# Turning pairs of fp16 as fp32 words, and setting the turns between matmuls, in a linear-attention and highway kernel

## The chip, the cores and the metric

The kernel runs on one core of a Trainium2 chip. A core has a matrix engine (TensorE, here PE, with its weight loads PEld), a vector engine (VectorE, DVE), a scalar engine (ScalarE, ACT), a general engine (GpSimd, POOL), a queue that issues transfers (SyncE, SP) and 16 DMA engines. The metric is the device time of one execution in microseconds, as the median of several runs.

## The reference

Eight batches of eight heads, 576 rows of 64 values each, go through linear attention; the result, 4608 rows of 512, goes through a highway layer with two 512 x 512 weights.

```
q_s = exp(q - max(q)) / sum(exp(q - max(q)))      # over the 64 values of a row
k_s = exp(k - max(k)) / sum(exp(k - max(k)))      # over the 576 rows
kv  = einsum('bhsd,bhse->bhde', k_s, v)
x   = einsum('bhsd,bhde->bhse', q_s, kv)          # then as 4608 rows of 512
H   = max(x @ w_h, 0)
T   = 1 / (1 + exp(-(x @ w_t + b_t)))
out = T * H + (1 - T) * x
```

Inputs and output are fp32.

## The kernel before

**Tiles.** The 4608 rows are cut into 36 tiles of 128 rows. Two batches make nine tiles: four of each batch, and one that holds the last 64-row groups of both. Tile numbers run from 0 to 35; tiles 31 to 34 belong to the last batch, number 7, and tile 35 to batches 6 and 7.

**Stages of a batch.** `ek` (ACT, line 253) writes exp(k) as fp16. `vc` (line 259) writes v as fp16, mostly on POOL. `kv` (line 269) multiplies them in 72 matmuls of 64 x 64 with 65 columns; the 65th column is a column of ones that gives the sum over rows. `kr` and `kn` (lines 281, 287) divide by that sum into a block matrix `kvb`. `eq` (ACT, lines 298 to 308) writes exp(q) as fp16 into `qe`, in the order position, head pair, value. `qt` (lines 310 to 327) turns `qe` on PE: a matmul of 128 columns with `is_transpose`, in which the data are the stationary operand, loaded by PEld, and an identity matrix is the moving one. The result goes to PSUM as fp16. `qc` (line 333) copies it to `eq`. Two of the three groups of batch 7 are turned by the DMA engines instead (`qd`, line 340).

**Stages of a tile.** `xu` (line 361): four matmuls of 130 columns of `eq` with `kvb`; two further columns carry the sums. `rs` and `x` (DVE, lines 370, 376) divide: `x` is the attention output, 128 rows of 512 in fp16. `xt` (line 384) turns `x` on PE, in four matmuls of 128 columns, each of which takes every second column of a block of 256; the result goes into the first half of the PSUM bank `turned`. `xe` (line 391) copies it to `xT`, on DVE or ACT. `bw` (lines 399, 401) puts the bias into a PSUM bank, by a copy on ACT or by a matmul. `mt` (line 411) adds x @ w_t to it and `mh` (line 419) forms x @ w_h, each in four matmuls of 512 columns with a quarter of `xT` as the stationary operand. `th` (lines 433, 435) is the gate's tanh on ACT; `dd` (DVE, line 439) forms max(x @ w_h, 0) - x in a scaled form (the identity is taken off w_h beforehand); `uu` multiplies, on DVE (line 453) or in two steps on POOL (lines 450, 451); `oo` adds x on POOL (line 471) and `st` stores.

Tiles 0, 4 and 5 take `xu`, `xt`, `xe` and the products in halves. At the start, `fill` runs matmuls on zeros (line 167) in the same bank `turned`.

**What sets the order.** A list of steps, `ORDER` (lines 16 to 62), names every step of the program, such as `xt_34_0` or `mh_34_0`; a suffix gives the engine. The loop at the end issues the steps in the list's order, and each engine works through its own part of them in that order; waits follow from the tiles that a step reads, writes or takes over. Loads and stores are all issued by SP but for three small ones, in that order too. Near the end the list reads (with "..." for steps left out):

```
xu_35_0 bw_32:A rs_35_0 oo_33_0 xt_34_0 mt_32_0 bw_34:A xe_34_0:D mh_34_0 st_33_0 x_35_0
xt_35_0 mt_34_0 dd_32 th_32_0 bw_35_1 oo_30_0 st_16_0 st_30_0 uu_32_0 xe_35_0 oo_32_0 mh_35_0
```

So on PE the turns of tile 34 are followed by the gate product of tile 32, and this by tile 34's own product `mh_34`, which needs the copy `xe_34`.

Of the kernel before, what the change touches and what calls it, by code (L numbers as in the profile page):

```python
# [8 lines left out]
FP32 = mybir.dt.float32  # L9
FP16 = mybir.dt.float16  # L10
AF = mybir.ActivationFunctionType
# [4 lines left out]
ORDER = """  # L16
# [49 lines left out]
def kernel(  # L66
# [10 lines left out]
    nc = tc.nc  # L77
    B, H, S, D = q.shape
    DM = H * D
    P = 128  # L80
    NP = 64
    NJ = S // NP
# [7 lines left out]
    qep = pool("qep", 2)  # L90
    eqp = pool("eqp", 4)
    xp = pool("xp", 6)
    xtp = pool("xtp", 3)
# [39 lines left out]
    def heads(i, k):  # L133
        return (k, k + 1) if i in HALVED else (0, 2)
# [39 lines left out]
    def landing(which, b):  # L174
        return once(f"{which}32{b}", lambda: ld.tile([P, 4, NJ * D], FP32, tag=which, name=f"{which}32_{b}"))
# [4 lines left out]
    def load_kv(which):  # L180
        def step(e, b, c):
            n = (2 if which == "k" else 1, 2)[b] if b < 2 else 4
            nc.sync.dma_start(landing(which, b)[:, c:c + n], rows_of(which, b)[:, c:c + n])
# [107 lines left out]

    GROUPS = ((0, 4), (4, 8), (8, 9))

    def eq(e, b, g):
        t = once(f"qe{b}", lambda: qep.tile([P, NJ, 4, D], FP16, tag="qe", name=f"qe_{b}"))
        if b in WIDE:
            if g == 2:
                nc.scalar.activation(t[:, 8], flat_q(b)[:, MAIN:].rearrange("p (c d) -> p c d", c=4), AF.Exp)
                return
            half = slice(0, 8) if e == "F" else slice(4 * g, 4 * g + 4)  # L300
            src = flat_q(b)[:, 0:MAIN].rearrange("p (c t d) -> p c t d", c=4, t=8)[:, :, half]
            nc.scalar.activation(t[:, half].rearrange("p t c d -> p c t d"), src, AF.Exp)
            return
        js, cs = slice(*GROUPS[g]), slice(0, 4)
        if b >= 2:
            js, cs = slice(0, NJ), slice(0, 4) if e == "F" else slice(2 * g, 2 * g + 2)
        nc.scalar.activation(t[:, js, cs].rearrange("p j c d -> p c j d"),  # L307
                             T[f"q32{b}"].rearrange("p c (j d) -> p c j d", j=NJ)[:, cs, js], AF.Exp)

    def qt(e, b, g):  # L310
        j0, j1 = GROUPS[g]
        a, s = (2, 2) if g < 2 else (1, 1)
        t = T[f"qps{b}_{g}"] = ps_q.tile([P, a, 4, s * NP], FP16, tag="qps", name=f"qps_{b}_{g}")
        if b in WIDE and g < 2:
            main = T[f"qe{b}"].rearrange("p j c d -> p (j c d)")[:, 0:MAIN]
            main = main.rearrange("p (hh j kk f) -> p j hh kk f", j=4, hh=2, kk=2)
            for jp in (2 * g, 2 * g + 1):
                for n in range(4):
                    nc.tensor.matmul(t[:, jp % 2, n], main[:, jp, n % 2, n // 2], idh,  # L319
                                     is_transpose=True, start=True, stop=True, skip_group_check=True)  # L320
            return
        for j in range(j0, j1):
            for kk in range(2):
                nc.tensor.matmul(  # L324
                    t[:, (j - j0) % 2, 2 * kk:2 * kk + 2].rearrange("p n (t s u) -> p n t s u", s=s, u=2)[:, :, :, (j - j0) // 2],
                    T[f"qe{b}"][:, j, 2 * kk:2 * kk + 2].rearrange("p c d -> p (c d)"), idh,
                    is_transpose=True, start=True, stop=True, skip_group_check=True)

    def qc(e, b, g):
        copy = nc.scalar.copy if e == "A" else nc.vector.tensor_copy  # L330
# [6 lines left out]
    def qd(e, b, g):  # L337
        t = T[f"eq{b}_{g}"] = eqp.tile([P, 2, 4, P], FP16, tag="eq", name=f"eq_{b}_{g}")
        half = MAIN // 2
        nc.sync.dma_start_transpose(t.rearrange("p a n t -> p (a n) t"),  # L340
                                    T[f"qe{b}"].rearrange("p j c d -> p (j c d)")[:, g * half:(g + 1) * half])
# [36 lines left out]

    def xt(e, i, k):
        k0, k1 = heads(i, k)  # L380
        t = T[f"xtps{i}"] = turned[:, 0]
        for n in range(2 * k0, 2 * k1):
            n0 = n // 2 * 2 * P
            nc.tensor.matmul(t[:, n], T[f"x{i}"][:, n0 + n % 2:n0 + 2 * P:2], idh, is_transpose=True,  # L384
                             start=True, stop=True, skip_group_check=True)

    def xe(e, i, k):
        k0, k1 = heads(i, k)
        t = once(f"xT{i}", lambda: xtp.tile([P, 4, P], FP16, tag="xT", name=f"xT_{i}"))
        copy = nc.vector.tensor_copy if e == "D" else nc.scalar.copy  # L390
        copy(t[:, 2 * k0:2 * k1], T[f"xtps{i}"][:, 2 * k0:2 * k1])  # L391


    def bw(e, i, h=0):
# [8 lines left out]
    def parts_of(i, k):  # L403
        return range(2 * k, 2 * k + 2) if i in HALVED else range(4)

    def mt(e, i, k):
        cs = columns(i, k)
        parts = parts_of(i, k)
        first = once(f"mt{i}", lambda: k) == k and len(parts) < 4
        for n in parts:  # L410
            nc.tensor.matmul(T[gate(i, k)][:, cs], T[f"xT{i}"][:, n], w16["t"][:, n, cs], start=False,  # L411
                             stop=(n == parts[-1] and not first), skip_group_check=True)

    def mh(e, i, k):
        first = f"gps{i}" not in T
        t = once(f"gps{i}", lambda: ps_g.tile([P, DM], FP32, tag="gps", name=f"gps_{i}"))
        parts = parts_of(i, k)
        for n in parts:
            nc.tensor.matmul(t, T[f"xT{i}"][:, n], w16["h"][:, n], start=(first and n == parts[0]),  # L419
                             stop=(n == parts[-1] and not (first and len(parts) < 4)), skip_group_check=True)  # L420


    LIFTED = {s.split(":")[0] for s in ORDER.split() if s.startswith("uu") and s[-2:] == ":P"}
# [49 lines left out]
    def st(e, i, h):  # L473
# [21 lines left out]
        setuppool=setup_pool, setupdve=setup_dve, bsplit=bsplit, fill=fill,  # L495
        k=load_kv("k"), v=load_kv("v"), q=load_q, w=load_w, b=load_b, bp=bp, bc=bc,
        wtc=wt_cast, whc=wh_cast, whd=wh_less_identity, ek=ek, vc=vc, kv=kv, kr=kr, kn=kn, eq=eq, qt=qt, qc=qc, qd=qd,
        xu=xu, rs=rs, x=x, xt=xt, xe=xe, bw=bw, mt=mt, mh=mh, th=th, dd=dd, uu=uu, oo=oo, st=st)
    with tc.manual_schedule():
        for step in ORDER.split():  # L500
            name, _, eng = step.partition(":")
            kind, *at = name.split("_")
            does[kind](eng, *(int(a) if a.isdigit() else a for a in at))


# [28 lines left out]
```

## Time and profile before

| | |
|---|---|
| median of 3 runs | 118.87 us (118.81 to 119.09) |
| span of the profiled execution | 116.9 us, 3424 instructions; no time of its own is listed beside the span |
| granted PE clock over the span | 0.995 |
| busy: PE, PEld | 109.5 us, 61.6 us |
| busy: DVE, ACT, POOL | 93.3, 90.0, 89.1 us |
| moved by DMA | 40.58 MB, 347 GB/s on the mean |
| turns on PE: of `x`, of queries | 144, and 80 + 48 |
| matmuls of the two products of 512 columns | 144 and 140 (and 8 of 256 columns) |

The span runs from the first to the last instruction of the program; what a run's time has beyond it lies before and after. Busy times of PE are those of overlapping matmuls: one that lasts 220 ns may be followed by the next after 55 ns. In a row of groups the fields are line, engine, operation, output <- inputs, shape and count, then the busy time and the mean of one in ns, then the idle time ahead of them with what ended it. In a timeline or a chain the first number is the start in us and the second the length.

### The profile page before, as it was taken

To read this page: it belongs to the slowest core of one execution; us is meant where nothing else is said; L and a number is where in the kernel's file an instruction comes from. 1 tells how busy PE (TensorE), PEld (TensorE's weight loads), DVE (VectorE), ACT (ScalarE), POOL (GpSimd) and SP (SyncE) were. 2 spreads that over 40 slices of the span, in tenths; PEclk is the share of its full clock that TensorE was granted. 3 is DMA by queue.
4 is the path that set the end of the run, shared out by engine and by line. 5 is a ranking of instruction groups with operands and counts; after the bars stand their busy time and mean duration, and the time that the engine had idled before them with its cause. 6 is when DMAs were issued, how large, how long until landed. Compare 5 with 4: busy or idle time off the path is not lost.

```text
span 116.9 us, 3424 instructions
## 1 busy us (share of the span) xinstructions
PE 109.5 (94%) x1351; PEld 61.6 (53%) x1351; DVE 93.3 (80%) x222; ACT 90.0 (77%) x132; POOL 89.1 (76%) x99
## 2 busy tenths in 40 slices
PE   5999987999999999999999999999999999999930
PEld 2354544545665656565665547566564555554520
DVE  5642587589799979979889798988989887899870
ACT  4356461897999999989999999998597998545520
POOL 5022237208996999999999999999989699999960
PEclk9999999999999999999999999999999999999998
DMA  2999999999999999999999999999999956992875
GB/s 42 399 392 377 408 398 385 375 377 379 393 391 397 383 391 393 358 375 387 357 376 360 387 392 363 390 381 383 399 398 217 302 204 270 397 404 115 315 295 179
DMA packets 24195, 40.58 MB, mean 347 GB/s; under 512 B 5362, under 2 KB 11762, under 8 KB 24180
## 3 DMA queue, kind: packets, MB, share of 16 engines
q1 hardware_dynamic: 24032, 40.24, 96.9%
q8 instruction: 10, 0.16, 0.6%
q10 hardware_dynamic: 148, 0.14, 0.4%
q14 instruction: 5, 0.04, 0.1%
HBM read 30.41 MB, written 9.44 MB: 341 GB/s over the span
## 4 chain that ended last, share of the span: by engine, by line
PE 67%; POOL 15%; issue 6%; DVE 5%; DMA 3%; SPq 1%; POOLq 0%; DVEq 0%
PE tps L411 18%; PE gps L419 16%; PE turned L167 9%; POOL o L471 7%; PE xu L361 6%; PE turned L384 5%; PE kv L269 5%; PE qps L324 4%; POOL u L451 4%; DMA out_dram<-o 3%; POOL g L450 2%; PE qps L319 2%; POOL v L259 2%; DVE x L376 2%; PE tps L401 1%
## 5 line engine op out<-in xcount | busy, mean ns | idle before, releaser
L471 POOL TENSOR_TENSOR o<-u,x 128x512 f32<-128x512 f16 (+1 forms) x36 | 40.6, 1143 | 1.6 <-DVE u L453 0.7
L411 PE MATMUL tps<-w16t,xT 128*128 128x512 f16 (+1 forms) x148 | 37.3, 373 | 0.0
L419 PE MATMUL gps<-w16h,xT 128*128 128x512 f16 x144 | 36.8, 379 | 0.5 <-DVE xT L391 0.5
L376 DVE TENSOR_TENSOR x<-xu,rs 128x512 f16<-128x512 f32 (+1 forms) x39 | 25.2, 649 | 2.4
L259 POOL CAST v<-v 128x1152 f16<-128x1152 f32 (+1 forms) x14 | 14.0, 1010 | 14.7 <-DMA v<-in_v_dram 13.7
L439 DVE SCALAR_TENSOR_TENSOR d<-x,gps 128x512 f16<-128x512 f16 x36 | 24.5, 680 | 0.3
L451 POOL TENSOR_TENSOR u<-g,d 128x512 f16<-128x512 f16 x17 | 19.7, 1158 | 1.7 <-DVE rs L370 0.4
L253 ACT ACTIVATE ek<-k 128x576 f16<-128x576 f32 (+2 forms) x15 | 17.9, 1225 | 3.0 <-DMA k<-in_k_dram 3.0
L419 PEld LDWEIGHTS <-xT 128*128 128x128 f16 x144 | 13.0, 98 | 12.3 <-DVE xT L391 1.8
L399 ACT COPY tps<-ball 128x512 f32<-128x512 f32 x28 | 16.6, 597 | 3.5 <-DVE u L453 3.2
L411 PEld LDWEIGHTS <-xT 128*128 128x128 f16 x148 | 13.2, 98 | 10.6 <-DVE xT L391 0.4
L361 PE MATMUL xu<-kvb,eq 128*128 128x130 f16 (+1 forms) x160 | 14.8, 224 | 0.2 <-DVE kvb L287 0.2
L384 PE MATMUL turned<-idh,x 128*128 128x128 f16 x144 | 14.2, 220 | 0.5 <-DVE x L376 0.5
L391 DVE COPY xT<-turned 128x512 f16<-128x512 f16 (+1 forms) x28 | 10.9, 391 | 4.2 <-PE turned L384 3.0
L435 ACT ACTIVATE tps<-tps 128x512 f32<-128x512 f32 (+1 forms) x20 | 11.2, 559 | 3.6 <-PE tps L411 3.3
L453 DVE SCALAR_TENSOR_TENSOR u<-tps,d 128x512 f16<-128x512 f32 (+1 forms) x19 | 12.7, 671 | 1.4 <-ACT tps L435 0.6
L361 PEld LDWEIGHTS <-eq 128*128 128x128 f16 (+1 forms) x160 | 10.0, 100 | 7.3 <-DVE x L376 2.5
L167 PE MATMUL turned<-blank 128*128 128x512 f16 x40 | 12.4, 458 | 1.5 <-POOL blank L149 1.3
L384 PEld LDWEIGHTS <-x 128*128 128x128 f16 x144 | 9.8, 98 | 6.0 <-DVE x L376 2.1
L307 ACT ACTIVATE qe<-q 128x1024 f16<-128x1024 f32 (+3 forms) x9 | 9.4, 1052 | 4.1 <-DMA q<-in_q_dram 4.1
L450 POOL TENSOR_SCALAR g<-th 128x512 f16<-128x512 f16 x17 | 10.6, 621 | 0.9 <-ACT th L433 0.9
L433 ACT ACTIVATE th<-tps 128x512 f16<-128x512 f32 x17 | 10.0, 594 | 0.9 <-PE tps L411 0.9
(48 smaller groups left out, 106.8 us busy)
## 6 DMA issues: line engine op xcount, KB each, us to landing
k<-in_k_dram SPq DMA_DIRECT2D x6, 1152.0 KB, 12.2
v<-in_v_dram SPq DMA_DIRECT2D x6, 1152.0 KB, 12.0
out_dram<-o SPq DMA_DIRECT2D x23, 256.0 KB, 4.0
q<-in_q_dram SPq DMA_DIRECT2D x10, 512.0 KB, 11.5
out_dram<-o SPq DMA_DIRECT2D x6, 512.0 KB, 3.8
k<-in_k_dram SPq DMA_DIRECT2D x4, 576.0 KB, 9.3
q<-in_q_dram SPq DMA_DIRECT2D x2, 1152.0 KB, 14.2
q<-in_q_dram SPq DMA_DIRECT2D x2, 640.0 KB, 10.5
```

Of the source, the lines that this page charges most:

```text
L167: nc.tensor.matmul(spare, blank[:, 0:P], blank, start=True, stop=True, skip_group_check=True)
L253: nc.scalar.activation(t[:, :, c:c + n].rearrange("p j c d -> p c j d"), T[f"k32{b}"][:, c:c + n].rearrange("p c (j d) -> p c j d", j=NJ), ...
L259: copy(v16[b % NV][:, c:c + n, :, 0:D], T[f"v32{b}"][:, c:c + n].rearrange("p c (j d) -> p c j d", j=NJ))
L361: nc.tensor.matmul(dst, turned_q(b, jp, n), kvb[b % NKV][:, hh, kk], start=True, stop=True, skip_group_check=True)
L376: nc.vector.tensor_mul(t[:, k0:k1], sums(i, k)[:, :, :, 0:64], T[f"rs{i}_{k}"][:, 0:k1 - k0].unsqueeze(3).to_broadcast([P, k1 - k0, 4, D]))
L384: nc.tensor.matmul(t[:, n], T[f"x{i}"][:, n0 + n % 2:n0 + 2 * P:2], idh, is_transpose=True, start=True, stop=True, skip_group_check=True)
L399: nc.scalar.copy(t[:, cs], ball[:, cs])
L411: nc.tensor.matmul(T[gate(i, k)][:, cs], T[f"xT{i}"][:, n], w16["t"][:, n, cs], start=False, stop=(n == parts[-1] and not first), skip_gro ...
L419: nc.tensor.matmul(t, T[f"xT{i}"][:, n], w16["h"][:, n], start=(first and n == parts[0]), stop=(n == parts[-1] and not (first and len(part ...
L439: nc.vector.scalar_tensor_tensor(t, T[f"x{i}"], -0.5, T[f"gps{i}"], op0=ALU.mult, op1=ALU.max)
L451: nc.gpsimd.tensor_mul(t, g, T[f"d{i}"])
L471: eng.tensor_add(t[:, cs], T[f"u{i}_{h}"][:, cs], T[f"x{i}"][:, cs])
```

## The change

Two neighbouring fp16 values fill one fp32 word. The turns now read the data as such words: one fp32 matmul with `is_transpose` of 128 columns, with the fp32 identity `idf`, replaces two fp16 ones.

For `x`, the columns of a block of 256 are 128 pairs, so `xt` issues two turns in place of four. Each word of the result holds two values; `xT` becomes [128, 2, 128, 2], its copy `xe` moves the same bytes in the same order of memory, and the products read their stationary operand with a step of two elements (`turned_x`).

For queries, `qe` is laid out so that the values of head pairs k = 0 and k = 1 alternate. `eq` therefore writes with a step of two elements. An instruction that wrote both head pairs in one becomes two, one for each k, except in the last position group (g = 2); these are groups 0 and 1 of batches 0 and 1, and the whole-batch instructions of batches 3 and 4. Batch 7's groups 0 and 1, turned by DMA, keep their layout. `qt` issues half as many turns, and `xu` reads `eq` with a step of two.

The turns of `x` are no longer issued by `xt` itself. They go into a list, and `mt` and `mh` issue one after each of their matmuls. A function looks from each `xt` step for the next `mt` or `mh`; if no other turn, `xu`, `qt`, `kv`, `fill`, `dd`, weight cast or bias matmul and no copy `xe` of another tile lies between, and the product's own bias copy doesn't either, that step is taken forward to stand right behind `xt`. If no product follows, both turns are issued at once.

```
     def eq(e, b, g):
+        exp = lambda dst, src: nc.scalar.activation(dst, src, AF.Exp)
+        pairs = flat_qe(b).rearrange("p (j w d k) -> p k w j d", j=NJ, w=2, k=2)
...
+        ks, js = (0, 1), slice(0, 8) if b in WIDE else slice(0, NJ)
+        if b >= 2:
+            ks = (0, 1) if e == "F" else (g,)
+        else:
+            js = slice(*GROUPS[g])
...
+        for k in ks:
+            exp(pairs[:, k, :, js], src[:, k, :, js])
     def qt(e, b, g):
...
+        q32 = flat_qe(b).bitcast(FP32).rearrange("p (j f) -> p j f", j=NJ)
+        t32 = t.rearrange("p a n t -> p (a n t)").bitcast(FP32).rearrange("p (a h t) -> p a h t", a=a, h=2)
+        turn = lambda dst, src: nc.tensor.matmul(dst, src, idf, is_transpose=True, start=True, stop=True,
+                                                 skip_group_check=True)
...
-            for kk in range(2):
-                nc.tensor.matmul(
...
+            turn(t32[:, (j - j0) % 2].rearrange("p h (t s u) -> p h t s u", s=s, u=2)[:, :, :, (j - j0) // 2], q32[:, j])
     def turned_q(b, jp, n):
...
-        return T[f"eq{b}_{jp // 2}"][:, jp % 2, n]
+        t = T[f"eq{b}_{jp // 2}"][:, jp % 2].rearrange("p n t -> p (n t)").rearrange("p (h t k) -> p h t k", h=2, k=2)
+        return t[:, n % 2, :, n // 2]
     def xt(e, i, k):
         k0, k1 = heads(i, k)
-        t = T[f"xtps{i}"] = turned[:, 0]
-        for n in range(2 * k0, 2 * k1):
-            n0 = n // 2 * 2 * P
-            nc.tensor.matmul(t[:, n], T[f"x{i}"][:, n0 + n % 2:n0 + 2 * P:2], idh, is_transpose=True,
-                             start=True, stop=True, skip_group_check=True)
+        T[f"xtps{i}"] = turned[:, 0].rearrange("p n t -> p (n t)").rearrange("p (c t r) -> p c t r", c=2, r=2)
+        pairs, turned_pairs = T[f"x{i}"].bitcast(FP32), spare[:, 0:2 * P].rearrange("p (c t) -> p c t", c=2)
+        for c in range(k0, k1):
+            waiting.append(lambda c=c: nc.tensor.matmul(
+                turned_pairs[:, c], pairs[:, c * P:(c + 1) * P], idf, is_transpose=True,
+                start=True, stop=True, skip_group_check=True))
...
+    def turned_x(i, n):
+        return T[f"xT{i}"][:, n // 2, :, n % 2]
...
+    def release(n=9):
+        for _ in range(min(n, len(waiting))):
+            waiting.pop(0)()
     def mt(e, i, k):
...
-            nc.tensor.matmul(T[gate(i, k)][:, cs], T[f"xT{i}"][:, n], w16["t"][:, n, cs], start=False,
+            nc.tensor.matmul(T[gate(i, k)][:, cs], turned_x(i, n), w16["t"][:, n, cs], start=False,
                              stop=(n == parts[-1] and not first), skip_group_check=True)
+            release(1)
+        release()
...
+    def laced(n):
+        for m in range(n + 1, len(steps)):
+            kind, at = steps[m].partition(":")[0].split("_")[0:2]
+            if kind in ("mt", "mh"):
+                return m
+            if kind in ("xt", "xu", "qt", "kv", "fill", "xe") and kind + "_" + at != "xe_" + steps[n].split("_")[1]:
+                return None
+            if kind == "dd" or (kind == "bw" and steps[m][-2:] != ":A") or kind in ("whc", "wtc"):
+                return None
+        return None
...
-        for step in ORDER.split():
+        while n < len(steps):
+            if steps[n].startswith("xt") and (m := laced(n)) is not None:
+                if f"bw_{steps[m].split('_')[1]}_0:A" not in steps[n:m] and f"bw_{steps[m].split('_')[1]}:A" not in steps[n:m]:
+                    steps.insert(n + 1, steps.pop(m))
...
+            if kind == "xt" and steps[n + 1].split("_")[0] not in ("mt", "mh"):
+                release()
```

`mh` is changed as `mt` is.

More of the change, by code (lines that the diff above doesn't have):

```diff
@@ L292, with flat_qe @@
     GROUPS = ((0, 4), (4, 8), (8, 9))
+    def flat_qe(b):
+        return once(f"qe{b}", lambda: qep.tile([P, NJ * 4 * D], FP16, tag="qe", name=f"qe_{b}"))
     def eq(e, b, g):
-        t = once(f"qe{b}", lambda: qep.tile([P, NJ, 4, D], FP16, tag="qe", name=f"qe_{b}"))
-        if b in WIDE:
[L297 to L302, printed above, removed]
-            return
[L304 to L308, printed above, removed]
+        exp = lambda dst, src: nc.scalar.activation(dst, src, AF.Exp)
+        pairs = flat_qe(b).rearrange("p (j w d k) -> p k w j d", j=NJ, w=2, k=2)
+        if b in WIDE and g == 2:
+            exp(pairs[:, :, :, 8], flat_q(b)[:, MAIN:].rearrange("p (k w d) -> p k w d", k=2, w=2))
+            return
+        if b in TURNED:
+            src = flat_q(b)[:, 0:MAIN].rearrange("p (c t d) -> p t c d", c=4, t=8)[:, 4 * g:4 * g + 4]
+            exp(flat_qe(b)[:, 0:MAIN].rearrange("p (t c d) -> p t c d", t=8, c=4)[:, 4 * g:4 * g + 4], src)
+            return
+        ks, js = (0, 1), slice(0, 8) if b in WIDE else slice(0, NJ)
[3 more added lines that the diff above has]
+            js = slice(*GROUPS[g])
+        if b in WIDE:
+            src = flat_q(b)[:, 0:MAIN].rearrange("p (k w j d) -> p k w j d", k=2, w=2, j=8)
+        else:
+            src = T[f"q32{b}"].rearrange("p (k w) (j d) -> p k w j d", k=2, j=NJ)
+        if b < 2 and g == 2:
+            exp(pairs[:, :, :, 8], src[:, :, :, 8])
+            return
+        for k in ks:
+            exp(pairs[:, k, :, js], src[:, k, :, js])
     def qt(e, b, g):
@@ L312, in qt @@
         a, s = (2, 2) if g < 2 else (1, 1)
+        q32 = flat_qe(b).bitcast(FP32).rearrange("p (j f) -> p j f", j=NJ)
         t = T[f"qps{b}_{g}"] = ps_q.tile([P, a, 4, s * NP], FP16, tag="qps", name=f"qps_{b}_{g}")
+        t32 = t.rearrange("p a n t -> p (a n t)").bitcast(FP32).rearrange("p (a h t) -> p a h t", a=a, h=2)
+        turn = lambda dst, src: nc.tensor.matmul(dst, src, idf, is_transpose=True, start=True, stop=True,
+                                                 skip_group_check=True)
         if b in WIDE and g < 2:
-            main = T[f"qe{b}"].rearrange("p j c d -> p (j c d)")[:, 0:MAIN]
-            main = main.rearrange("p (hh j kk f) -> p j hh kk f", j=4, hh=2, kk=2)
             for jp in (2 * g, 2 * g + 1):
-                for n in range(4):
-                    nc.tensor.matmul(t[:, jp % 2, n], main[:, jp, n % 2, n // 2], idh,
-                                     is_transpose=True, start=True, stop=True, skip_group_check=True)
+                for hh in range(2):
+                    turn(t32[:, jp % 2, hh], q32[:, 4 * hh + jp])
             return
         for j in range(j0, j1):
-            for kk in range(2):
[L324 to L327, printed above, removed]
+            turn(t32[:, (j - j0) % 2].rearrange("p h (t s u) -> p h t s u", s=s, u=2)[:, :, :, (j - j0) // 2], q32[:, j])
     def qc(e, b, g):
@@ L380, in xt @@
         k0, k1 = heads(i, k)
-        t = T[f"xtps{i}"] = turned[:, 0]
-        for n in range(2 * k0, 2 * k1):
-            n0 = n // 2 * 2 * P
-            nc.tensor.matmul(t[:, n], T[f"x{i}"][:, n0 + n % 2:n0 + 2 * P:2], idh, is_transpose=True,
-                             start=True, stop=True, skip_group_check=True)
+        T[f"xtps{i}"] = turned[:, 0].rearrange("p n t -> p (n t)").rearrange("p (c t r) -> p c t r", c=2, r=2)
[4 more added lines that the diff above has]
+                start=True, stop=True, skip_group_check=True))
     def xe(e, i, k):
         k0, k1 = heads(i, k)
-        t = once(f"xT{i}", lambda: xtp.tile([P, 4, P], FP16, tag="xT", name=f"xT_{i}"))
+        t = once(f"xT{i}", lambda: xtp.tile([P, 2, P, 2], FP16, tag="xT", name=f"xT_{i}"))
         copy = nc.vector.tensor_copy if e == "D" else nc.scalar.copy
-        copy(t[:, 2 * k0:2 * k1], T[f"xtps{i}"][:, 2 * k0:2 * k1])
+        copy(t[:, k0:k1].rearrange("p c t r -> p (c t r)"),
+             T[f"xtps{i}"][:, k0:k1].rearrange("p c t r -> p (c t r)"))
+    def turned_x(i, n):
+        return T[f"xT{i}"][:, n // 2, :, n % 2]
     def bw(e, i, h=0):
@@ L404, in parts_of @@
         return range(2 * k, 2 * k + 2) if i in HALVED else range(4)
+    waiting = []
+    def release(n=9):
+        for _ in range(min(n, len(waiting))):
+            waiting.pop(0)()
     def mt(e, i, k):
@@ L418, in mh @@
         for n in parts:
-            nc.tensor.matmul(t, T[f"xT{i}"][:, n], w16["h"][:, n], start=(first and n == parts[0]),
+            nc.tensor.matmul(t, turned_x(i, n), w16["h"][:, n], start=(first and n == parts[0]),
                              stop=(n == parts[-1] and not (first and len(parts) < 4)), skip_group_check=True)
+            release(1)
+        release()
     LIFTED = {s.split(":")[0] for s in ORDER.split() if s.startswith("uu") and s[-2:] == ":P"}
@@ L498 @@
         xu=xu, rs=rs, x=x, xt=xt, xe=xe, bw=bw, mt=mt, mh=mh, th=th, dd=dd, uu=uu, oo=oo, st=st)
-    with tc.manual_schedule():
-        for step in ORDER.split():
-            name, _, eng = step.partition(":")
+    steps = ORDER.split()
+    def laced(n):
[8 more added lines that the diff above has]
+        return None
+    with tc.manual_schedule():
+        n = 0
+        while n < len(steps):
+            if steps[n].startswith("xt") and (m := laced(n)) is not None:
+                if f"bw_{steps[m].split('_')[1]}_0:A" not in steps[n:m] and f"bw_{steps[m].split('_')[1]}:A" not in steps[n:m]:
+                    steps.insert(n + 1, steps.pop(m))
+            name, _, eng = steps[n].partition(":")
             kind, *at = name.split("_")
             does[kind](eng, *(int(a) if a.isdigit() else a for a in at))
+            if kind == "xt" and steps[n + 1].split("_")[0] not in ("mt", "mh"):
+                release()
+            n += 1
 _INS = ['q', 'k', 'v', 'moe_w_h', 'moe_w_t', 'moe_b_t']
```

2 lines of the change are left out of this document (1 added, 1 removed).

## The prediction, made before the change was run

> **What bounds the kernel now.** I read the page's busy shares and slices first, then the table by stretches, the groups by shape, the chain of work that ended last, and last the timelines of the queues around the end of the loads. Shares and slices (a digit is tenths of a slice of 2.9 us):
>
> ```profile
> PE 109.5 (94%) x1351; PEld 61.6 (53%) x1351; DVE 93.3 (80%) x222; ACT 90.0 (77%) x132; POOL 89.1 (76%) x99
> PE   5999987999999999999999999999999999999930
> POOL 5022237208996999999999999999989699999960
> DMA  2999999999999999999999999999999956992875
> 50.00:60.00 10.00, 9.99 (x156) 6.05 (x155) 8.78 (x21) 9.80 (x13) 9.76 (x11) 1.00 1.07 375
> 80.00:90.00 10.00, 9.99 (x88) 5.82 (x87) 9.12 (x20) 7.62 (x12) 9.44 (x11) 1.00 1.10 350
> 90.00:100.00 10.00, 10.00 (x143) 5.80 (x142) 8.30 (x19) 9.38 (x18) 8.70 (x10) 1.00 0.85 269
> ```
>
> In the last three rows the columns after the length are the busy us of PE, PEld, DVE, ACT and POOL, then granted clock, DMA share and GB/s. PE has no gap from 20 us on, at full clock. But it is not alone: until 90 us the DMA engines are full as well (share 1.07 and 1.10), and POOL is busy 9.4 to 9.8 us in 10. Whatever PE gains has to pass both.
>
> How far the loads allow more is seen at the last load of k. SP issues it at 77.69, it needs 11.5 us to land (the row of that one transfer), and ACT uses it at 90.11:
>
> ```profile
> 77.69 0.59 SPq L183 DMA_DIRECT2D k<-in_k_dram  x1
> DMA to landing us min/median/max: 11.5/11.5/11.5
> 90.11 2.12 ACT L253 ACTIVATE ek<-k 128x2304 f16<-128x2304 f32 x1
> 92.13 0.58 ACT L433 ACTIVATE th<-tps 128x512 f16<-128x512 f32 x1
> 92.80 0.62 POOL L450 TENSOR_SCALAR g<-th 128x512 f16<-128x512 f16 x1 [0.89 <-ACT th L433]
> 92.80:113.43 20.63, 19.29 (x207) 10.88 (x206) 17.68 (x37) 13.25 (x27) 19.09 (x19) 1.00 0.77 292
> ```
>
> It lands at 77.69 + 11.5 = 89.2, so the exponential of the last batch can start at most 90.1 - 89.2 = 0.9 us earlier, and the `th` behind it on ACT, for which POOL sits idle 0.89 us, likewise. From 92.80 to the end of its last work POOL is busy 19.09 of 20.63 us. So a faster PE is worth at most 0.9 us before that point, and at most 20.63 - 19.09 = 1.5 us after it; the floor is 118.87 - 2.4 = 116.5, and lower only if the loads themselves become faster, which the change does not touch.
>
> **What a turn costs now.** Groups by shape, then three pieces of the chain, in which the second number is the time from one piece's start to the next one's:
>
> ```profile
> L384 PE MATMUL turned<-idh,x 128*128 128x128 f16 x144 | 14.2, 220 | 0.5 <-DVE x L376 0.5
> L324 PE MATMUL qps<-idh,qe 128*128 128x128 f16 x80 | 7.1, 220 | 0.0
> L319 PE MATMUL qps<-idh,qe 128*128 128x128 f16 x48 | 3.7, 219 | 0.0
> L384 PEld LDWEIGHTS <-x 128*128 128x128 f16 x144 | 9.8, 98 | 6.0 <-DVE x L376 2.1
> L411 PEld LDWEIGHTS <-xT 128*128 128x128 f16 x148 | 13.2, 98 | 10.6 <-DVE xT L391 0.4
> 62.51 0.22 PE turned L384 x4
> 62.73 0.86 PE tps L411 x4
> 70.69 0.45 PE qps L319 x8
> ```
>
> Four turns take 0.22 us of PE's queue and eight 0.45, so 55.5 ns each though one lasts 220: they are pipelined, and the load of 98 ns lies under the work before it. A product of 512 columns takes 0.86 / 4 = 216 ns. All turns together hold PE for (144 + 80 + 48) x 55.5 ns = 15.1 us.
>
> **The change, part by part.**
>
> Half as many turns. 272 fp16 turns become 72 for x and 64 for queries, in fp32. Following the list of steps by the new rule for lacing, 32 of x's 72 come between matmuls (17 steps), 40 stay back to back, and all 64 for queries stay back to back.
>
> The price of one fp32 turn is in no row. Low end: 55.5 ns, that of an fp16 turn of the same 128 columns. High end: 4 x 55.5 = 222 ns, which is also what one unpipelined turn lasts (220). For one behind a matmul of 216 ns I take 55.5, since even a load of 98 ns fits under 216. For those back to back I take 98: the load is the nearest row for what could stick out when the data are four bytes wide, and it is longer than the 55 ns turn ahead of it. Then PE needs 32 x 55.5 + 104 x 98 ns = 12.0 us, 3.1 less than 15.1; at the low end 7.5, which is 7.6 less; at 222 back to back 24.9, 9.8 more.
>
> The Trainium skill, "TensorE: Matmul & The Clock Gate", bears on this twice. Its Terms say that the transpose mode made fp32 four times faster on trn2, which speaks for the low end. Its section "Weight-path perf modes — Fast Weight Load (FWL) and DoubleRow" says that the fast weight load is off for fp32, which speaks against the change; with the load that the page gives without it, 128 / 1.2 = 107 ns, the sum would be an estimated 32 x 55.5 + 104 x 107 = 12.9 us, 2.2 less. No run here has an fp32 turn, so neither is shown.
>
> Stationary operands with a step. `xT` and `eq` are now read with a step of two elements. That is free: the present turns already load `x` with that step, 98 ns, as long as the load of `xT` without one.
>
> The exponential of queries. Two batches' parts, and the whole-batch ones of batches 3 and 4, become two instructions each; the output has a step of 4 bytes:
>
> ```profile
> L302 ACT ACTIVATE qe<-q 128x1024 f16<-128x1024 f32 x6 | 6.4, 1061 | 0.0
> L302 ACT ACTIVATE qe<-q 128x2048 f16<-128x2048 f32 x1 | 1.9, 1919 | 0.0
> L307 ACT ACTIVATE qe<-q 128x2304 f16<-128x2304 f32 x1 | 2.1, 2127 | 0.0
> L307 ACT ACTIVATE qe<-q 128x1152 f16<-128x1152 f32 x2 | 2.3, 1154 | 0.0
> L433 ACT ACTIVATE th<-tps 128x512 f16<-128x512 f32 x17 | 10.0, 594 | 0.9 <-PE tps L411 0.9
> L435 ACT ACTIVATE tps<-tps 128x512 f32<-128x512 f32 x18 | 10.4, 580 | 2.5 <-PE tps L411 2.4
> ```
>
> Batches 0 and 1: 4 x (2 x 594 - 1061) = 0.5 us, before 30 us. Batch 3: 2 x 1154 - 2127 = 0.18; batch 4: 2 x 1061 - 1919 = 0.20. ACT has 0.2 us idle in the quoted ten, so some 0.2 of this may show if the loads do not cover it; I count 0 and keep +0.4 for the range. The step itself I take as free: an output of 4-byte elements (580) costs no more than one of 2 bytes (594).
>
> Lacing. On PE nothing changes place, except that the first matmul of the next product goes ahead of the turns. Ten `mt` or `mh` steps are taken forward in the list to get there; they issue matmuls alone, no DMA, and pass only steps of ACT, DVE, POOL and SP, whose queues stay as they are. That the first matmul no longer stands behind a turn's wait for `x` is worth up to the 0.5 us in the L384 row; I count 0, as it is one wait early in the run. What it costs is the copy `xT` that waits for the second turn. Before, the last of four turns starts 0.17 us after the first; now the second starts after two matmuls and a turn, 216 + 55 + 216 = 0.49. The copy comes 0.32 us later, and the product that needs it follows one product later in four places (steps xt_9, xt_23, xt_32, xt_34), and little more in xt_35. Two of them before, and the last:
>
> ```profile
> 105.50 0.64 PEld L419 LDWEIGHTS <-xT 128*128 128x128 f16 x4 [0.22 <-DVE xT L391]
> 106.92 0.40 PE L384 MATMUL turned<-idh,x 128*128 128x128 f16 x4
> 107.16 1.03 PE L411 MATMUL tps<-w16t,xT 128*128 128x512 f16 x4
> 107.49 0.37 DVE L391 COPY xT<-turned 128x512 f16<-128x512 f16 x1
> 107.92 0.63 PEld L419 LDWEIGHTS <-xT 128*128 128x128 f16 x4 [0.23 <-DVE xT L391]
> 108.02 1.03 PE L419 MATMUL gps<-w16h,xT 128*128 128x512 f16 x4
> 109.31 0.59 ACT L391 COPY xT<-turned 128x512 f16<-128x512 f16 x1 [0.51 <-PE turned L384]
> ```
>
> The load for mh_34 already waits for the copy, with all of PE's queue behind it, and nothing is left over: the product starts at 108.02, as the one before ends (107.16 + 0.86). After: the second turn starts at 106.92 + 0.49 = 107.41 and ends at 107.63, the copy at 108.08, the product starts near 108.2, 0.2 later than before. The same reading gives 0.17 for mh_32 (its load waits at 105.50 now) and 0.24 for mh_35 (copy on ACT, 0.59). In the end phase, where PE has no cover, lacing costs 0.6 us in these three. POOL's only other waits there are short, so nothing hides it.
>
> **Sum**, against the profiled execution (span 116.9; the median of the runs is 118.87, so 1.96 us lie around the span, and I add changes to the median). Before 92.8 us: PE gains about 2.6 of its 3.1, of which the loads let 0.9 through: -0.9. After: xt_28 laced -0.11, three back to back (4 x 55.5 - 2 x 98 = 0.026 each) -0.08, two queries' turns -0.03, the three late copies +0.6: +0.4. Together -0.5: 118.87 - 0.5 = **118.3 to 118.4; I write 118.3**. With 55.5 for all, the three back to back give -0.33 and the end phase +0.1: 118.1. If the late copies cost nothing there either, it is -0.9 - 7 x 0.11 - 0.11 = -1.8: 117.1.
>
> **Rivals.**
> (1) *A turn back to back costs more than it replaces*: slower. Its place is the 104 turns without a matmul ahead, 96 of them before 92.8 us. For: four-byte data, and PE without any gap, so each ns counts. Against: nothing measured. The 24 laced ones before 92.8 save 24 x 55.5 = 1.3, less 2 x 0.28 for xt_9 and xt_23: 0.8. It decides at 111 + 800 / 96 = 119 ns, where that is used up and the end phase leaves +0.4: 119.3. If load and turn come one after the other, 98 + 55 = 153: 96 x 42 ns = 4.0, less 0.8, with 0.4 + 8 x 0.042 at the end: +3.9, 122.8. At 222: 96 x 111 ns = 10.7, less 0.8, plus 1.3: +11, 130. The page's rule on fast weight load is this mechanism in words.
> (2) *Nothing to be seen*: the loads set the pace to 90 us and let less than 0.9 through, as another load on the way has less room, and the late copies take back the rest: 118.6 to 119.3.
> (3) *ACT's output step costs*: if the price per element doubled (about 0.85 us more per 1024), five batches of 2304 would add 9.6 us to an engine that is 98% busy: some 127. The row of 580 against 594 speaks against it.
>
> **How the numbers follow.** Forecast case (a turn up to 110 ns) 0.43, its own range 117.1 to 118.7; rival 1 0.36; rival 2 0.14; rival 3 0.07. Of the forecast case 0.07 lies within 0.3% of no change (118.5 to 119.2, about what a measurement can tell), of rival 2 0.10, the rest of it slower. So faster 0.36, same 0.17, slower 0.36 + 0.07 + 0.04 = 0.47. The range starts at 117.1 and must reach into rival 1, past its middle value: 124 leaves out its upper third and rival 3, 0.19.
>
> **What would show it.** The pace of the new turns in the chain: two back to back in about 0.2 us, four for queries in about 0.4; a laced product in 0.97 us for its six instructions. ACT's `ek` of the last batch starting at its landing, near 89.2, with a wait for the DMA. Waits of PE's loads for `xT` of 0.2 us or more at mh_32, mh_34 and mh_35. I am wrong if four queries' turns take over 0.5 us, if the last `ek` starts later than 90.1, or if it starts much earlier than 89.2.

## The result, and the profile after

The changed kernel takes 122.27 us (median of 4 runs, 122.20 to 122.43) against 118.93 us of the kernel before on the same chip: 1.0288 times, with a 95% interval of 1.0267 to 1.0309. It is slower by 3.3 us, inside the stated range but on the other side of the forecast of 118.3. Its profiled execution has a span of 120.4 us, 3.5 more than before.

The shares, one of the slices and two rows of the table by stretches, as quoted of before:

```profile
PE 111.3 (92%) x1215; PEld 61.9 (51%) x1215; DVE 94.1 (78%) x222; ACT 94.6 (79%) x138; POOL 89.1 (74%) x99
PE   5999778989999999999999999999999999999950
50.00:60.00 10.00, 9.78 (x112) 5.90 (x99) 8.37 (x20) 9.72 (x14) 9.76 (x11) 1.00 1.07 375
80.00:90.00 10.00, 9.90 (x71) 5.58 (x69) 8.76 (x19) 8.32 (x12) 8.28 (x9) 1.00 1.11 349
```

PE has 136 matmuls fewer (1215 for 1351) and yet is busy 1.8 us longer, in a span 3.5 us longer. ACT has six instructions more and is busy 4.6 us longer. The groups by shape say why:

```profile
L394 PE MATMUL turned<-idf,x 128*128 128x128 f32 x72 | 16.9, 278 | 0.6 <-DVE x L386 0.5
L394 PEld LDWEIGHTS turned<-idf,x 128*128 128x128 f32 x72 | 9.4, 141 | 5.2 <-DVE x L386 1.6 <-ACT xT L402 0.9 <-issue 0.2
L328 PE MATMUL qps<-idf,qe 128*128 128x128 f32 x64 | 11.2, 282 | 0.8 <-ACT qe L298 0.7
L298 ACT ACTIVATE qe<-q 128x1024 f16<-128x1024 f32 x8 | 10.3, 1302 | 0.0
L298 ACT ACTIVATE qe<-q 128x1152 f16<-128x1152 f32 x4 | 5.9, 1500 | 0.0
L298 ACT ACTIVATE qe<-q 128x512 f16<-128x512 f32 x8 | 5.6, 766 | 4.3 <-DMA q<-in_q_dram 4.3
```

An fp32 turn lasts 278 ns for 220, and its load 141 for 98. The exponential of 1152 queries takes 1500 ns for 1154. The row of 1024 mixes two kinds: one by one in the trace, the six that are written with the step take 1343 to 1435 ns, and the two of batch 7, which keep the old layout, 1053 and 1062, as long as the 1061 of before. What a turn takes of PE's queue is read in pieces of the chain, from one start to the next: back to back, laced, and four of queries.

```profile
47.92 0.11 PE turned L394
48.03 0.21 PE tps L432
48.24 0.11 PE turned L394
48.35 0.43 PE tps L432 x2
...
74.32 0.22 PE turned L394 x2
...
88.58 0.44 PE qps L328 x4
```

It is 110 ns in all three, just twice the 55.5 of an fp16 turn. So nothing is saved by halving their number, laced or not. Where PE's queue had run dry, and often behind short matmuls, the first of several turns holds it for some 165 ns and the following ones for 110; in this row four of queries hold PE from 74.72 to the next start at 75.21, 0.49 us:

```profile
74.72 0.66 PE L328 MATMUL qps<-idf,qe 128*128 128x128 f32 x4
75.21 1.03 PE L442 MATMUL gps<-w16h,xT 128*128 128x512 f16 x4
```

Where the time is lost: the last batch's product `kv` started at 92.80 in the kernel before and starts at 95.65 now. These are rows of two timelines, before first:

```profile
92.80 0.78 PE L269 MATMUL kv<-v,ek 64*64 64x65 f16 x72
```

```profile
92.95 2.12 ACT L253 ACTIVATE ek<-k 128x2304 f16<-128x2304 f32 x1
95.65 0.78 PE L269 MATMUL kv<-v,ek 64*64 64x65 f16 x72
```

That is 2.85 us by then. From there to the end of the span it is 120.4 - 95.65 = 24.75 us for 116.9 - 92.80 = 24.1: 0.65 more. So most of the loss lies before the end phase. Who waited longer shows in the waits (engine, line, what ended the wait; total us, times, longest), before and after:

```profile
DVE xT L391 <- PE turned L384: 3.0, 7, 0.8
PEld L419 <- DVE xT L391: 1.8, 4, 1.0
PEld L324 <- ACT qe L307: 0.6, 1, 0.6
```

```profile
DVE xT L402 <- PE turned L394: 6.9, 12, 1.0
PEld L442 <- DVE xT L402: 3.5, 7, 1.0
PEld qps L328 <- ACT qe L298: 3.2, 6, 0.9
```

The copies wait 3.9 us longer for the turns, the loads for the products 1.7 us longer for the copies, and the turns of queries 2.6 us longer for ACT. The runs below take these apart.

### The profile page after: what moved, and what is told of

The parts are those of the page before. It is cut to its first block, busy times and chain, and to the rows that moved or that the text cites. A ratio compares the mean times of both kernels' runs of the same rounds, so it can differ in the third digit from the quotient of the medians.

```text
span 120.4 us, 3165 instructions
## 1 busy us (share of the span) xinstructions
PE 111.3 (92%) x1215; PEld 61.9 (51%) x1215; DVE 94.1 (78%) x222; ACT 94.6 (79%) x138; POOL 89.1 (74%) x99
## 4 chain that ended last, share of the span: by engine, by line
PE 58%; DMA 22%; ACT 12%; DVE 3%; issue 1%; SPq 1%; DVEq 0%
PE gps L442 19%; PE tps L432 19%; DMA q<-in_q_dram 14%; DMA w32h<-in_moe_w_h_dram 8%; ACT qe L298 7%; PE turned L394 6%; PE qps L328 5%; PE xu L371 5%; PE kv L269 4%; DVE xT L402 1%; ACT xT L402 1%; ACT eq L342 1%; ACT th L458 1%; ACT tps L414 1%; ACT tps L460 1%
## 5 line engine op out<-in xcount | busy, mean ns | idle before, releaser
L432 PE MATMUL tps<-w16t,xT 128*128 128x512 f16 (+1 forms) x148 | 39.4, 374 | 0.1
L442 PE MATMUL gps<-w16h,xT 128*128 128x512 f16 x144 | 38.2, 380 | 0.9 <-DVE xT L402 0.5
L298 ACT ACTIVATE qe<-q 128x512 f16<-128x512 f32 (+3 forms) x26 | 24.4, 981 | 4.3 <-DMA q<-in_q_dram 4.3
L442 PEld LDWEIGHTS <-xT 128*128 128x128 f16 x144 | 13.2, 98 | 14.4 <-DVE xT L402 3.5
L432 PEld LDWEIGHTS <-xT 128*128 128x128 f16 x148 | 14.1, 99 | 10.8 <-DVE xT L402 0.8
L394 PE MATMUL turned<-idf,x 128*128 128x128 f32 x72 | 16.9, 278 | 0.6 <-DVE x L386 0.5
L371 PEld LDWEIGHTS <-eq 128*128 128x128 f16 (+1 forms) x160 | 10.5, 101 | 8.0 <-DVE x L386 2.9
L167 PE MATMUL turned<-blank 128*128 128x512 f16 x40 | 11.3, 426 | 1.5 <-POOL blank L149 1.3
L394 PEld LDWEIGHTS turned<-idf,x 128*128 128x128 f32 x72 | 9.4, 141 | 5.2 <-DVE x L386 1.6
L328 PE MATMUL qps<-idf,qe 128*128 128x128 f32 x64 | 11.2, 282 | 0.8 <-ACT qe L298 0.7
```

Source lines behind the costliest of these rows:

```text
L298: exp = lambda dst, src: nc.scalar.activation(dst, src, AF.Exp)
L328: turn = lambda dst, src: nc.tensor.matmul(dst, src, idf, is_transpose=True, start=True, stop=True, skip_group_check=True)
L394: waiting.append(lambda c=c: nc.tensor.matmul(turned_pairs[:, c], pairs[:, c * P:(c + 1) * P], idf, is_transpose=True, start=True, stop=Tr ...
L432: nc.tensor.matmul(T[gate(i, k)][:, cs], turned_x(i, n), w16["t"][:, n, cs], start=False, stop=(n == parts[-1] and not first), skip_group_ ...
L442: nc.tensor.matmul(t, turned_x(i, n), w16["h"][:, n], start=(first and n == parts[0]), stop=(n == parts[-1] and not (first and len(parts) ...
```

## The experiments

Ratios are to the kernel before on the same chip; a per cent is 1.19 us.

| run | what it holds of the change | median us | ratio (95%) |
|---|---|---|---|
| changed kernel | all | 122.27 | 1.0288 (1.0267 to 1.0309) |
| e1 | x in pairs, laced | 121.10 | 1.0203 (1.0186 to 1.0220) |
| e2 | all but lacing | 120.32 | 1.0140 (1.0125 to 1.0155) |
| e3 | queries' part | 120.07 | 1.0114 (1.0099 to 1.0129) |
| e4 | exp(q) with its step, fp16 turns | 119.62 | 1.0077 (1.0059 to 1.0095) |
| e5 | x in pairs, not laced | 119.48 | 1.0040 (1.0019 to 1.0061) |
| e6 | lacing, fp16 turns | 120.89 | 1.0154 (1.0125 to 1.0183) |
| e7 | all but the step (and the pieces) of exp(q) | 121.12 | 1.0197 (1.0180 to 1.0215) |
| e8 | e1, both turns behind one matmul | 119.49 | 1.0044 (1.0023 to 1.0065) |
| e9 | exp(q) in more pieces, no step | 118.82 | 0.9973 (0.9951 to 0.9995) |
| e9, 5 rounds | the same | 118.79 | 0.9994 (0.9984 to 1.0005) |
| e10 | e1, lacing at ten steps with long cover | 119.74 | 1.0078 (1.0062 to 1.0094) |
| e11 | e1, lacing at seven steps with short cover | 120.41 | 1.0134 (1.0117 to 1.0151) |

**Which part costs: e1 to e4.** My first theory after the result was A, that ACT's longer exponentials are the main loss; its rival was B, the late copies of the lacing. Theory C put the queries' loss on PE.

e1 gives `eq`, `qt`, `qd` and `turned_q` of the kernel before back to the changed kernel. e2 takes the lacing out:

```
-            if steps[n].startswith("xt") and (m := laced(n)) is not None:
-                if ...:
-                    steps.insert(n + 1, steps.pop(m))
...
-            if kind == "xt" and steps[n + 1].split("_")[0] not in ("mt", "mh"):
+            if kind == "xt":
                 release()
```

e3 gives the changed kernel's `eq`, `qt`, `qd` and `turned_q` to the kernel before, with x as it was. e4 takes of these only `eq`, and reads its interleaved values for fp16 turns:

```
+        words = flat_qe(b).rearrange("p (j f k) -> p j f k", j=NJ, k=2)
...
-                    T[f"qe{b}"][:, j, 2 * kk:2 * kk + 2].rearrange("p c d -> p (c d)"), idh,
+                    words[:, j, :, kk], idh,
```

> The changed kernel with the queries' part undone: exp(q) in the old order, queries turned in fp16; x still turned as pairs and laced. Theory A (the output step of exp(q) on ACT, 982 to 1302 ns and more per instruction, makes ACT the bound between 30 and 80 us; fp32 turns of 110 ns are neutral): only the late copies of the lacing are left, about +0.6 us on 118.9, so 119.3 to 119.9. Theory B (lacing delays the copies of the turned x all along the run and that is the whole loss): no change against the changed kernel, 122.0 to 122.5.

> The changed kernel with both turns of x issued at once, in the old order of steps; queries as changed. Theory A: the +2.8 us that stand at the last batch's product stay, the +0.6 of the end phase goes: 121.4 to 121.9. Theory B: back to 118.7 to 119.2.

> The kernel before with the queries' part alone: exp(q) written with a step, queries turned as fp32 pairs; x as before, no lacing. Theory A: 121.2 to 121.9, as without lacing. Theory B: 118.7 to 119.2.

> The kernel before with only the new order of exp(q): written with a step of two elements and in more instructions, then turned in fp16 as before, the turns reading with a step of two. Theory A: as e3, 121.2 to 121.9, since two fp16 turns cost what one fp32 turn costs. Theory C (fp32 turns of queries cost PE more than the two they replace, and ACT is hidden): 118.7 to 119.2.

Measured: 121.10, 120.32, 120.07, 119.62. None of the theories holds alone. Without the queries' part 2.0% stay, where A had 0.5%; without lacing 1.4% stay, where B had none. Lacing is the larger half: the changed kernel less e2 is 1.0288 - 1.0140 = 1.5%. The step of exp(q) is 0.8% (e4), and turning queries as fp32 on top of it another 0.4% (e3 less e4), which is C's part.

**Pieces or step: e9.** Theory A's cost could come from the extra instructions or from the step. e9 writes the same pieces without it, and turns in fp16:

```
-        pairs = flat_qe(b).rearrange("p (j w d k) -> p k w j d", j=NJ, w=2, k=2)
+        pairs = flat_qe(b).rearrange("p (j k w d) -> p k w j d", j=NJ, w=2, k=2)
...
```

> The kernel before with exp(q) cut into the changed kernel's instructions, but written without a step, and turned in fp16. It separates the two parts of run e4 (+0.9). If the step costs (0.24 to 0.3 ns per element): 118.7 to 119.1. If the extra instructions cost: 119.4 to 119.8.

> Run e9 again with more rounds: exp(q) of the kernel before in smaller instructions, no step. e9 gave 0.9973 (0.9951 to 0.9995) beside a scattered series of the kernel before. If the gain is real: 0.996 to 0.999; if it was that scatter: 0.999 to 1.002.

Measured: 0.9973 in a scattered series, then 0.9994 (0.9984 to 1.0005): no difference. So it is the step of the write; that e4's turns also read with a step costs nothing, as their loads take 98 ns like those of before. The same instructions with it and without it, groups by shape of e4 and then of e9, and the row of each for 30 to 90 us (busy us of PE, PEld, DVE, ACT, POOL):

```profile
L298 ACT ACTIVATE qe<-q 128x1024 f16<-128x1024 f32 x8 | 10.2, 1291 | 0.0
L298 ACT ACTIVATE qe<-q 128x1152 f16<-128x1152 f32 x4 | 5.8, 1505 | 0.0
L298 ACT ACTIVATE qe<-q 128x512 f16<-128x512 f32 x8 | 5.6, 763 | 4.2 <-DMA q<-in_q_dram 4.2
30.00:90.00 60.00, 59.98 (x830) 35.89 (x828) 52.63 (x118) 58.25 (x79) 56.10 (x57) 1.00 1.07 376
```

```profile
L298 ACT ACTIVATE qe<-q 128x1024 f16<-128x1024 f32 x8 | 8.4, 1062 | 0.0
L298 ACT ACTIVATE qe<-q 128x1152 f16<-128x1152 f32 x4 | 4.5, 1156 | 0.0
L298 ACT ACTIVATE qe<-q 128x512 f16<-128x512 f32 x8 | 4.6, 621 | 4.3 <-DMA q<-in_q_dram 4.3
30.00:90.00 60.00, 59.98 (x832) 35.80 (x829) 53.02 (x120) 56.16 (x79) 57.04 (x58) 1.00 1.07 376
```

The row of 1024 again holds batch 7's two without the step. Two rows of e4's timeline, one of each kind:

```profile
69.95 1.37 ACT L298 ACTIVATE qe<-q 128x1024 f16<-128x1024 f32 x1
83.03 1.05 ACT L298 ACTIVATE qe<-q 128x1024 f16<-128x1024 f32 x1
```

The six with the step take 1369 ns on the mean, and the same six of e9 1063. So the step costs (1369 - 1063) / 1024 = 0.30 ns, (1505 - 1156) / 1152 = 0.30 ns and (763 - 621) / 512 = 0.28 ns per element. ACT goes from 56.2 to 58.3 of 60 us, and POOL does 0.9 us less in the same stretch. Over the whole run the step adds 4.8 us to these groups and the smaller ones of 256 (25.4 us for 20.5); 0.9 us of it reach the end.

**The parts of x: e5, e6, e8.** e5 is the kernel before with pairs of x, turned at once. e6 laces the kernel before's own fp16 turns, two behind each matmul, with everything else as it was:

```
+            waiting.append(lambda n=n, n0=n0: nc.tensor.matmul(
+                t[:, n], T[f"x{i}"][:, n0 + n % 2:n0 + 2 * P:2], idh, is_transpose=True, ...
...
+            release(2)
```

e8 is e1 with `release(2)` for `release(1)`: both fp32 turns stand behind the first matmul.

> The kernel before with x alone turned as fp32 pairs, two turns back to back, no lacing, queries as before. If a 110 ns turn simply replaces two of 55.5 ns: 118.7 to 119.1, no change. If the turn's longer way (278 against 220 ns) reaches the copies that wait for it: up to 0.06 us for each copy that PE waits for, 119.0 to 119.4.

> The kernel before with lacing alone: four fp16 turns, two behind each of the next product's first two matmuls, the list of steps taken forward as in the changed kernel. If the late copies are the cause of what lacing costs (theory B, for 2.0 to 2.4 of the 3.3 us): 120.7 to 121.2, as with x in pairs. If the fp32 turn between fp16 matmuls is the cause (a switch of type on PE): 118.7 to 119.3.

> The kernel of run e1 with both turns behind the first matmul of the product instead of one behind each of the first two: the last turn starts 0.33 us after the step's start instead of 0.49 (before: 0.17), so the copy is 0.16 us late instead of 0.32. Late copies as the cause: about half of e1's +2.4, 119.7 to 120.4. Cause in the steps taken forward, or in the interruption of the product: no change against e1, 120.9 to 121.3.

Measured: 1.0040, 1.0154, 1.0044. e6 settles that lacing costs by itself, 1.5%, with no fp32 word in the kernel; a switch of type on PE has no part in it. e8 shows that neither the steps taken forward nor the interrupted product does it: the steps stay forward and the product is interrupted, if once and not twice (in the chain above an interrupted product takes just what its pieces hold: 0.11, 0.21, 0.11 and 0.43 us), but the last turn starts 0.33 us after the step's first matmul (216 + 110 ns) and not 0.54 (216 + 110 + 216), and the loss is that of the pairs alone. With 110 ns a turn and not the 55 that the expectation went by, the last turn ends 0.21 us later than before in e8 and 0.43 later in e1; it is 0.43 in e6 too, with fp16 turns. The cost fell by more than the half I expected, so it does not grow evenly with the delay; the rows of tile 34 below show why. The pairs alone cost 0.4%. In their profile a pair holds PE from 85.04 to 85.31 where four fp16 turns did from 84.43 to 84.67, 0.27 for 0.24 us. Rows of e5's timeline and of before's:

```profile
85.04 0.44 PE L384 MATMUL turned<-idf,x 128*128 128x128 f32 x2
85.31 1.03 PE L417 MATMUL tps<-w16t,xT 128*128 128x512 f16 x4
```

```profile
84.43 0.40 PE L384 MATMUL turned<-idh,x 128*128 128x128 f16 x4
84.67 1.03 PE L411 MATMUL tps<-w16t,xT 128*128 128x512 f16 x4
```

**Where lacing costs: e10, e11.** The loop of e1 is limited to steps with much other work on PE between the second turn and the product that needs the copy (e10), or with `in` for `not in` to those with little (e11):

```
+    SHORT = ("xt_0_0", "xt_9_0", "xt_18_0", "xt_23_0", "xt_32_0", "xt_34_0", "xt_35_0")
...
-            if steps[n].startswith("xt") and (m := laced(n)) is not None:
+            if steps[n].startswith("xt") and steps[n] not in SHORT and (m := laced(n)) is not None:
...
```

> The kernel of run e1 (x in pairs, queries as before, lacing) with lacing only at the ten steps after which PE has at least 0.97 us of other work left behind the second turn before the product that needs the copy. If lacing costs through the seven steps with less than 0.7 us of such work (theory D: PE waits for the late copy), nothing is left but the price of the pairs: 119.2 to 119.6. If late copies cost because they hold up DVE and ACT, whatever PE has to do (theory E): over half of the 1.9 us between e5 and e1 stays, 120.3 to 121.

> The kernel of run e1 with lacing only at the other seven steps (xt_0_0, xt_9, xt_18, xt_23, xt_32, xt_34, xt_35). Theory D: nearly all of e1's loss, 120.7 to 121.2. Theory E: less than half of it, 119.6 to 120.3.

Measured: 1.0078 and 1.0134. Against 1.0040 of the pairs without lacing, the ten steps with long cover cost 0.4% and the seven with short cover 0.9%, together 1.3 of the 1.6% between e5 and e1. Theory D (PE waits for the late copy) has the larger part; both results fall between the two ranges, so something else has a part; that it is the held-up queues of DVE and ACT (E) is what is left of my theories, and was not shown. One of the seven in the timeline of the changed kernel, the one that the prediction worked out for tile 34:

```profile
110.20 0.39 PE L432 MATMUL tps<-w16t,xT 128*128 128x512 f16 x1
110.75 0.27 PE L394 MATMUL turned<-idf,x 128*128 128x128 f32 x1
110.86 0.59 PE L432 MATMUL tps<-w16t,xT 128*128 128x512 f16 x2
111.06 0.42 DVE L402 COPY xT<-turned 128x512 f16<-128x512 f16 x1
111.54 0.55 PEld L442 LDWEIGHTS <-xT 128*128 128x128 f16 x4 [0.58 <-DVE xT L402]
111.54 1.04 PE L442 MATMUL gps<-w16h,xT 128*128 128x512 f16 x4
```

From the first instruction of the two interleaved steps to tile 34's own product it takes 111.54 - 110.20 = 1.34 us; before, in the rows that the prediction shows, 108.02 - 106.92 = 1.10. The second turn is issued at 110.75, the last two matmuls end their part of the queue at 110.86 + 2 x 0.216 = 111.29, and PE then waits 0.25 us for the copy. PE stops like this at four more products of the changed kernel. These are the loads that wait there:

```profile
44.62 0.55 PEld L442 LDWEIGHTS <-xT 128*128 128x128 f16 x4 [0.58 <-DVE xT L402]
84.50 0.55 PEld L432 LDWEIGHTS <-xT 128*128 128x128 f16 x4 [0.58 <-DVE xT L402]
108.86 0.55 PEld L442 LDWEIGHTS <-xT 128*128 128x128 f16 x4 [0.58 <-DVE xT L402]
113.90 0.55 PEld L442 LDWEIGHTS <-xT 128*128 128x128 f16 x4 [0.52 <-ACT xT L402]
```

They belong to xt_9, xt_23, xt_32 and xt_35. The idle time of a load counts from the end of the load before it, so it is longer than PE's stop: from start to start of the matmuls PE loses 0.25 us at each of the first three, as at tile 34, and 0.30 at the last: 1.3 us in the five places. e1, e6 and e11 have the same five stops; the kernel before, e5 and e10 have none of them. Of the 1.9 us by which e1 is slower than e5 (1.6%) theory D thus has some 1.3 us in sight, and e11's 0.9%, 1.1 us, agrees; the 0.4% of the ten long-cover steps is not among these stops.

In e8 the same five stops take 0.03 to 0.04 us, and 0.08 at the last, as here at tile 34:

```profile
108.23 0.39 PE L422 MATMUL tps<-w16t,xT 128*128 128x512 f16 x1
108.46 0.38 PE L384 MATMUL turned<-idf,x 128*128 128x128 f32 x2
108.68 0.81 PE L422 MATMUL tps<-w16t,xT 128*128 128x512 f16 x3
109.36 0.39 PE L432 MATMUL gps<-w16h,xT 128*128 128x512 f16 x1
```

That is 109.36 - 108.23 = 1.13 us for the 1.34 of the changed kernel and the 1.10 of before. A delay of 0.43 us makes PE wait 0.25 and one of 0.21 makes it wait 0.03, so these products had some 0.18 us to spare; only what goes beyond that is lost. This is why half the delay cost so little.

**The step under lacing: e7.** The changed kernel with the exponential of the kernel before:

```
+        t = flat_qe(b).rearrange("p (j c d) -> p j c d", j=NJ, c=4)
...
```

> The changed kernel with exp(q) written as in the kernel before (one piece, no step). Queries are then turned with the wrong values paired, so the output is not the reference's; the work of PE, DVE, POOL and the DMA queues is that of the changed kernel. If the step's 0.9 us add to the rest: 122.3 - 0.9 = 121.4 (121.1 to 121.7). If ACT's extra time is hidden once lacing holds the kernel up: 122.0 to 122.4.

Measured: 121.12, so the step is worth 1.15 us in the full change too (1.0288 - 1.0197 = 0.9%). It equals e1 (121.10): with lacing in place, queries in fp32 pairs cost nothing that can be seen, for the 0.4% that they cost without it.

The parts add up: pairs of x 0.4, lacing 1.5 to 1.6, the step 0.8 to 0.9, queries' turns 0 to 0.4, together 2.7 to 3.3% against 2.9% measured.

## Why the prediction was wrong

- *What bounds the kernel*: right as far as it went. PE was full, and so were POOL and, as the step showed, ACT. The bound by the loads, 0.9 us, was never reached: the last `ek` starts at 92.95 and its load lands near 89.2, so nothing here tests it.
- *The price of a turn* is the first step that failed. I took 55.5 ns behind a matmul and 98 back to back, and so 3.1 us less on PE, of which 0.9 were to come through. It is 110 ns in both places, so 136 of them hold PE for 15.0 us where the old ones held it for 15.1, and the saving is zero. The reasoning that the load decides was wrong: the load did grow, to 141 ns, yet a laced turn with 216 ns to hide it costs the same 110. My threshold in rival 1, 119 ns, rested on laced turns at 55.5, so a price below it did not make the change a gain. The rule on fast weight load of the Trainium skill ("TensorE: Matmul & The Clock Gate", "Weight-path perf modes — Fast Weight Load (FWL) and DoubleRow") says that it is off for fp32, and the trace agrees with a longer load, 141 for 98; that load sets no pace behind a matmul of 216 ns. The 107 ns that I took as the load without it stand on that page of the Trainium skill as the price of a load in general; the trace has 141. Of "four times faster" in its Terms nothing can be checked, as no run has a slower fp32 form; against fp16 the turn is two times slower.
- *The output step of exp(q)*, taken as free, is the second. The row that I leaned on (580 ns for fp32 results against 594 for fp16 ones) compares widths of elements that lie side by side, not a step. It costs 0.28 to 0.30 ns per element, 0.9 to 1.15 us in the run. Rival 3 named it, with a price of 0.85 us per 1024 elements, where 0.31 were measured, and a chance of 0.07.
- *Lacing*: the mechanism was right, and so was its place in the end phase: +0.65 us from the last `kv` on for the 0.6 foreseen, and 0.24 at tile 34 for 0.2. It is lacing that does it: this stretch takes 24.7 to 24.8 us in the changed kernel, e1, e6, e7 and e11, which have these late turns, and 24.1 to 24.3 in all others, e8 among them. That the size fits is in part luck, since the turns come 0.43 us late and not 0.32, and PE's three stops there are 0.25, 0.25 and 0.30. The term was mis-sized because I charged it there only. Before 92.8 us I set it against a gain of PE that did not exist; the short-cover steps cost there as well, 0.25 us each at 44.62 and 84.50, and the ten with long cover were counted as free and cost 0.4%. By itself lacing costs 1.8 us (e6).
- *Extra instructions on ACT* at nothing: right, 0.9994. *Stationary operands with a step*: the loads of `eq` and `xT` still take 98 to 99 ns.
- *The sum*: -0.5 us was forecast and +3.3 measured. Of the 3.8 between them the gain of PE that is not there makes 0.9 before the last batch and 0.2 after it; lacing beyond its 0.6 makes 1.2, the step of exp(q) 0.9 to 1.15, the pairs of x 0.5 (e5), and the queries' turns up to 0.4.
- *The signs*: one that I was wrong came true, as the last `ek` starts at 92.95, later than 90.1. Four queries' turns stay under 0.5 us (0.44 and 0.49 in the rows above), and the loads for `mh_32`, `mh_34` and `mh_35` wait for `xT` as foretold.
- *Rivals*: none held alone. Of rival 1 the direction held without its price, of rival 3 the place held with a third of its price, and what I had put into the forecast case as a small term, lacing, was the largest cost.

Not settled: where the 0.4% of the ten long-cover steps goes, and whether the pairs' 0.4% is the 165 ns of first turns, which no run takes out. That a turn lasts 58 ns longer is not the reason: back to back, the second fp32 turn starts 110 ns after the first and the fourth fp16 turn 167 ns, so both ways end 0.39 us after the first start (110 + 278, 167 + 220).

## What to carry to other kernels

Before fewer, wider instructions are counted as a saving, measure one of them in its place: here two fp16 turns and one fp32 turn held the engine for the same 110 ns. When a layout is changed for one engine, price the new access pattern on the engine that writes it, above all if that engine has four idle microseconds in sixty, as ACT had. Work put between the halves of a producer delays its consumer; in a kernel with every queue full, count that delay at each consumer with little other work ahead of it, less what that work covers (0.18 us here), and not in the end phase alone. Before the mean of a row in a profile is used as a price, see whether all its instructions are of the same kind.

## What the runs showed of the hardware that I had not expected

- An fp32 turn of 128 x 128 holds PE for 110 ns, laced or back to back, and lasts 272 to 282; the fp16 one 55.5 and 220. The first of several after a pause, and often after short matmuls, holds it for some 165.
- ACT's exponential with an fp16 output at a step of two elements takes 0.28 to 0.30 ns per element longer than side by side (1369 for 1063 ns at 1024 elements, e4 and e9).
- The last turn ending 0.43 us later cost 1.5 to 1.6% (e6; e1 less e5); 0.21 us later cost nothing that could be measured (e8 less e5). At five products PE stopped for 1.3 us in the first case and 0.2 in the second.
